# The passage between two layers of a decode kernel: one load moved ahead, one load reshaped, and idle matmuls added

## The chip, the cores and the metric

The kernel runs on one core of a Trainium2 chip. The metric is the device time of one execution in microseconds. A core has five engines with instruction streams of their own: TensorE (PE in the profile, with its weight loads as PEld), VectorE (DVE), ScalarE (ACT), GpSimd (POOL) and SyncE (SP). Sixteen DMA engines bring data from the device's memory (HBM) into the on-chip memory SBUF; here SP issues most of the transfers and ACT a few. TensorE writes its results into PSUM. Engines wait for each other, and for transfers, by semaphores.

## The reference

The reference is one decode step (one token) through two layers that use the same weights and the same caches. A layer is attention over a cache of 8192 keys and values with 32 heads, then an MLP with ReLU; each works on the layer-normed input and adds to the residual.

```python
B, Sq, D = 1, 1, 640
H, Sk, Dh = 32, 8192, 128        # caches: (1, 32, 8192, 128), f32, one for K and one for V
Dff = 1728

def _A_ref(x, k_cache, v_cache, wq, wo):
    q = (x @ wq).reshape(B, Sq, H, Dh).transpose(0, 2, 1, 3)
    scores = einsum("bhqd,bhkd->bhqk", q, k_cache) * (Dh ** -0.5)
    o = einsum("bhqk,bhkd->bhqd", softmax(scores), v_cache)
    return o.transpose(0, 2, 1, 3).reshape(B, Sq, H * Dh) @ wo

def _B_ref(x, w1, w2):
    return maximum(x @ w1, 0) @ w2

x = A_x
x = x + _A_ref(_layernorm(x), A_k_cache, A_v_cache, A_wq, A_wo)
x = x + _B_ref(_layernorm(x), B_w1, B_w2)
x = x + _A_ref(_layernorm(x), A_k_cache, A_v_cache, A_wq, A_wo)   # same caches, same weights
x = x + _B_ref(_layernorm(x), B_w1, B_w2)
```

K and V of one head are 4 MB each, 268 MB for all heads. They don't fit on chip, so almost all of them is read once in each layer.

## The kernel before, in words

**Heads and their data.** Layer 1 takes the heads 0 to 31 in order. Layer 2 takes 31 down to 24 first, then the others (`HEADS`). K and V come in units of 32 KB to 6 MB, laid out in memory one after the other in the order in which they are loaded. Some units of the heads 29, 30 and 31 stay on chip from layer 1 to layer 2 (`kept`).

**The ring and the planner.** `ring` is one large SBUF tile. `place` finds room for the next unit, `pump` issues loads on SP's queue as long as there is room, and `release` (called behind the last matmul that reads a piece) frees the room and calls `pump`. So loads run ahead of the computing by what the ring holds. When `pump` has issued the last unit of a layer it also issues W2's blocks 0 to 7 into `by_parts`, an area behind the ring.

**Other tiles that are lent.** Between the layers four units of head 29 are loaded into tiles that serve something else at other times: `load_beside(0)` into `mix` (864 KB), `load_beside(1)` into `wct` (320 KB), `load_beside(2)` and `load_beside(3)` into the two halves of `by_parts` (1280 KB each). Each is issued on SP's queue where the last reader of the tile stands in the program (lines 887 to 909).

**One head.** `begun` computes the scores (`scores`, line 494; the query is spread over a small tile by `spread_column`, line 482). `largest` (line 506) and `exponentials` (lines 511 to 520) form the softmax's numerators: a reduction on VectorE, a small matmul, a second reduction, and the exponential on ScalarE into the tile "p". `turn` (line 527) transposes them on VectorE, `values` (line 545) multiplies them with V, and `output` (lines 562 to 586) gathers one column. Work that isn't urgent (queries of the next group, the output projection) is put between by `side_work`.

**The MLP between the layers.** `mlp` starts from the last head's output `o`. The hidden row is completed by a product with `mix` (line 645), copied out (into `hr` and `hr_2`), turned into columns `hT`, and multiplied with W2 in 14 blocks of up to 128 rows (`product`, line 861, through `times_rows`, line 463). Block 13 has 64 rows (`W2_LAST`). In layer 1 the blocks 8 to 13 are loaded late, since their room has to come free: 8 and 9 into `mix` after line 820, the others into `by_parts` over the blocks 0 to 3, each after the product that reads the overwritten block (lines 866 to 868). Then x2, the input of layer 2, is formed (line 918). It is turned into columns (`columns`, line 923), the first head's query is computed from it without waiting for the layer norm (line 929), turned (line 941) and spread (line 942), and the scores of layer 2's first head begin. The norm's mean (`mean`, line 343) and deviation follow beside them.

**Idle matmuls.** `in_wait(n)` (line 387) is a matmul of n columns whose result nobody reads. The kernel before has a few of them, at places where TensorE waits.

What sets the order is the program as written: each engine runs its instructions in program order, and SP issues its loads in program order, each when its semaphores allow.

Of the kernel before, what the change touches and what calls it, by code (L numbers as in the profile page):

```python
# [10 lines left out]
F32 = mybir.dt.float32  # L11
# [4 lines left out]
P = 128  # L16
# [96 lines left out]
W2_MORE = [(SLOTS, 10), (10, 12), (12, 13), (13, FB)]  # L113
W2_LAST = 2 * (F_ROWS[2] - P * F_TILES)


@with_exitstack
def decode_kernel(ctx: ExitStack, tc: tile.TileContext, x, kv, wq, wo, wqo, w1, w2, out):
# [33 lines left out]
    def w2_block(L, b):  # L152
        if b < SLOTS:
            return w2_t[:, b]
        if L:
            return w2_rest[0][:, b - SLOTS]
        return mix[:, (b - SLOTS) * D :][:, :D] if b < 10 else w2_t[:, b - 10]
# [20 lines left out]
    def pump():  # L178
        while todo:
# [21 lines left out]
        n = (FB - SLOTS) * D // 8  # L201
        if not w2_rest:
            at = place(1, (0, None), n)
            if at is not None:
                w2_rest.append(ring[:, 8 * at : 8 * (at + n)].rearrange("p (b d) -> p b d", d=D))
                for a, b in W2_MORE:
                    part_of_w2(a, b, w2_rest[0][:, a - SLOTS : b - SLOTS])

    def part_of_w2(a, b, where):
        rows = W2_LAST if a == FB - 1 else P  # L210
        part = w2[P * D * a : P * D * b].rearrange("(p b d) -> p b d", p=P, d=D)
        nc.sync.dma_start(where[:rows], part[:rows])
# [129 lines left out]
    def mean(pt, s):  # L342
        nc.tensor.matmul(pt[:, 5:6], all_rows, s, start=True, stop=True)

    def less_mean(pt, cols):
        m = work.tile([P, 1], F32, name="ln_m")
        nc.vector.tensor_scalar(m, pt[:, 5:6], 1.0 / D, 0.0, op0=ALU.mult, op1=ALU.add)
# [306 lines left out]
    def attention_and_mlp(L, xr, s, before=None):  # L654
# [112 lines left out]
        for where, h in enumerate(heads):  # L767
# [49 lines left out]
    def mlp(L, o, last, xp, ph):  # L817
# [3 lines left out]
        if L == 0:  # L821
            part_of_w2(SLOTS, 10, mix[:, : 2 * D].rearrange("p (b d) -> p b d", d=D))
# [4 lines left out]
        hr = wct.rearrange("p c d -> p (c d)")[:, : 2 * P]  # L827
# [51 lines left out]
        for g in range(2):  # L879
# [3 lines left out]
                sel[:, 2 + g : 3 + g],  # L883
# [3 lines left out]
        if L == 0:  # L887
            load_beside(1, wct.rearrange("p c d -> p (c d)"), NB * P)
# [4 lines left out]
            hT[: 2 * half, nb + 1 : nb + 2], pj[: 2 * half, 1:2], 0.0, 0.0, op0=ALU.max, op1=ALU.add  # L893
# [28 lines left out]
        in_wait(64)  # L922
        pt = columns(x2)
        cols = work.tile([P, NB], F32, name="x_cols")
# [14 lines left out]
        mean(pt, s2)  # L939
        turned = ps_m.tile([P, 512], F32, name="acc")  # L940
        nc.tensor.matmul(turned[:, :1], row, one_of_each, start=True, stop=True)
# [35 lines left out]
def _laid_out(A_x, A_k_cache, A_v_cache, A_wq, A_wo, B_w1, B_w2):  # L977
# [21 lines left out]
    for b, f in enumerate(_hidden_rows()):  # L999
        w2[f >= 0, b] = np.asarray(B_w2)[f[f >= 0]][:, _COLS]  # L1000

# [13 lines left out]
        "w2": np.concatenate([w2[:, a:b].reshape(-1) for a, b in W2_PARTS + W2_MORE]),  # L1015
# [25 lines left out]
```

## Time and profile before

| | us |
|---|---|
| median of 3 runs | 1348.46 |
| lowest, highest | 1348.38, 1349.58 |
| the profiled execution | 1348.99 |
| its span, first to last instruction | 1347.2 |
| TensorE busy (matmuls) | 893.9 (66%) |
| VectorE busy | 297.2 (22%) |
| ScalarE busy | 58.5 (4%) |
| mean granted clock of TensorE | 0.794 |
| moved by DMA | 573.05 MB, mean 425 GB/s |

How to read the profile: times are in microseconds from the first instruction. The page shows the busy share of each engine in 40 equal slices, the clock granted to TensorE in tenths of full speed, and what the DMA engines moved in GB/s. The chain that ended last is followed back from the last instruction, at each step to what released it. In a view by stretches a row shows the stretch, its length, the busy time of PE, PEld, DVE, ACT and POOL with their instruction counts, then the granted clock, the DMA engines' busy share and GB/s. In the timeline a row shows start, length, engine, line, operation and tiles, how many instructions are merged, and in brackets the idle time before and what ended it.

The passage from layer 1 to layer 2 lies at about 690 to 710 us: the last head's output column is there at 692.6 us (line 586), x2 at 703.4 (line 918), and the first scores of layer 2 begin at 707.0 (line 494).

### The profile page before, as it was taken

What the parts mean: (1) busy time and instruction counts of PE and PEld (TensorE: products, weight loads), DVE (VectorE), ACT (ScalarE), POOL (GpSimd) and SP (SyncE); (2) the same over time, 40 slices, a digit from 0 to 9 for tenths busy, and PEclk for the clock granted to TensorE, in tenths of its full rate; (3) what the DMA queues carried; (4) which work ended last, traced back from release to release, by engine and by line L of the source; (5) the groups of instructions that cost most, each with busy time, mean ns of one, the idle gap of its engine ahead of it and who ended that gap; (6) DMA issues with size and microseconds to landing.
All of it is one profiled execution on the core that took longest, in us unless ns stands there. A gap on an engine that the chain in (4) does not pass through costs nothing.

```text
span 1347.2 us, 13967 instructions
## 1 busy us (share of the span) xinstructions
PE 893.9 (66%) x6092; PEld 271.7 (20%) x6092; DVE 297.2 (22%) x979; ACT 58.5 (4%) x147; POOL 2.9 (0%) x10
## 2 busy tenths in 40 slices
PE   5463676757657657576788666667576775767667
PEld 2121121211112112122243211212122121112123
DVE  2120131211212112122123322122121212212222
ACT  0000000000000000000000000000000000000000
POOL 0000000000000000000000000000000000000000
PEclk9776797888777778778798887678768778687789
DMA  9999999999999999999999999999999999999997
GB/s 398 434 427 431 435 441 428 425 429 440 431 433 424 432 437 426 433 423 421 429 364 410 435 432 434 430 435 426 435 436 426 437 429 431 435 429 430 426 427 330
DMA packets 24277, 573.05 MB, mean 425 GB/s; under 512 B 2836, under 2 KB 2968, under 8 KB 6168
## 3 DMA queue, kind: packets, MB, share of 16 engines
q1 hardware_dynamic: 21192, 530.62, 92.0%
q10 hardware_dynamic: 3024, 41.53, 7.3%
q8 instruction: 48, 0.79, 0.2%
q14 instruction: 13, 0.11, 0.0%
HBM read 572.15 MB, written 0.00 MB: 425 GB/s over the span
## 4 chain that ended last, share of the span: by engine, by line
DMA 66%; PE 27%; DVE 4%; ACT 1%; issue 1%; SPq 0%; ACTq 0%; DVEq 0%
DMA ring<-in_kv 63%; PE outs L545 10%; PE ps L494 10%; DMA ring<-in_w 2%; DVE p L566 1%; DVE h_t L506 1%; ACT p L520 1%; PE px L632 1%; PE pm L511 1%; PE acc L463 1%; PE pm L532 1%; PE px L421 1%; DMA both_t<-in_kv 1%; PE pm L579 1%; DVE p L527 1%
## 5 line engine op out<-in xcount | busy, mean ns | idle before, releaser
L545 PE MATMUL outs<-ring,p 128*4 128x512 f32 (+2 forms) x2160 | 345.5, 764 | 175.2 <-DMA ring<-in_kv 105.9
L494 PE MATMUL ps<-ring,spread_q 128*32 128x512 f32 (+3 forms) x2088 | 327.6, 723 | 122.4 <-DMA ring<-in_kv 121.7
L506 DVE TENSOR_REDUCE h_t<-ps 128x1 f32<-128x512 f32 x64 | 44.3, 692 | 385.2 <-PE ps L494 385.1
L494 PEld LDWEIGHTS ps<-ring,spread_q 128*32 128x32 f32 x2088 | 66.3, 125 | 255.6 <-issue 168.7
L545 PEld LDWEIGHTS outs<-ring,p 128*4 128x4 f32 x2160 | 49.0, 94 | 339.5 <-issue 198.5
L520 ACT ACTIVATE p<-ps,h_t 128x512 f32<-128x512 f32 x63 | 43.3, 687 | 1180.6 <-DVE h_t L512 1180.6
L527 DVE STREAM_TRANSPOSE p<-p 128x128 f32<-128x128 f32 x256 | 79.8, 312 | 63.6 <-ACT p L520 57.0
L579 PE MATMUL pm<-ones,p 128*128 128x1 f32 (+1 forms) x128 | 25.7, 270 | 97.4 <-DVE p L566 97.4
L562 DVE TENSOR_SCALAR p<-outs,ind 128x128 f32<-128x128 f32 x64 | 22.4, 351 | 284.0 <-PE outs L545 284.0
L566 DVE SCALAR_TENSOR_TENSOR p<-outs,ind,p 128x128 f32<-128x128 f32 x188 | 66.0, 351 | 6.7
L511 PE MATMUL pm<-ident,h_t 128*128 128x128 f32 x128 | 32.3, 335 | 40.4 <-DVE h_t L506 40.3
L579 PEld LDWEIGHTS pm<-ones,p 128*128 128x128 f32 x128 | 20.3, 199 | 164.0 <-DVE p L566 163.1
L632 PE MATMUL px<-w_t,wct 128*128 128x448 f32 (+1 forms) x80 | 45.8, 659 | 0.0
L532 PEld LDWEIGHTS pm<-ind,h_t 128*128 128x128 f32 x128 | 27.0, 263 | 79.8 <-issue 79.8
L433 DVE TENSOR_SCALAR q_row<-px,ln_r 128x128 f32<-128x128 f32 x56 | 19.5, 348 | 95.5 <-PE ps L494 54.6
L511 PEld LDWEIGHTS pm<-ident,h_t 128*128 128x128 f32 x128 | 19.8, 194 | 88.6 <-DVE h_t L506 86.8
L535 DVE RECIPROCAL h_t<-pm 128x1 f32<-128x1 f32 x64 | 10.7, 168 | 99.3 <-PE pm L532 99.3
L532 PE MATMUL pm<-ind,h_t 128*128 128x1 f32 x128 | 32.5, 323 | 0.0
L421 PE MATMUL px<-both_t,ln_xc 128*32 128x512 f32 x140 | 30.8, 706 | 0.0
L435 PEld LDWEIGHTS px<-sel,q_row 128*128 128x128 f32 x112 | 20.0, 223 | 37.5 <-DVE q_row L433 30.9
L463 PE MATMUL acc<-both_t,o_cols 128*32 128x160 f32 x488 | 27.0, 372 | 0.0
L512 DVE TENSOR_REDUCE h_t<-pm 128x1 f32<-128x128 f32 x64 | 18.7, 292 | 35.0 <-PE pm L511 35.0
(126 smaller groups left out, 227.3 us busy)
## 6 DMA issues: line engine op xcount, KB each, us to landing
ring<-in_kv SPq DMA_DIRECT2D x50, 6144.0 KB, 35.2
ring<-in_kv SPq DMA_DIRECT2D x24, 4096.0 KB, 30.3
ring<-in_kv SPq DMA_DIRECT2D x29, 2048.0 KB, 28.9
both_t<-in_wqo ACTq DMA_DIRECT2D x12, 2560.0 KB, 24.6
ring<-in_kv SPq DMA_DIRECT2D x4, 5120.0 KB, 33.6
ring<-in_kv SPq DMA_DIRECT2D x9, 1024.0 KB, 24.0
ring<-in_kv SPq DMA_DIRECT2D x4, 1280.0 KB, 10.7
ring<-in_w SPq DMA_DIRECT2D x4, 1280.0 KB, 26.8
```

What stands on the lines that cost most here:

```text
L421: nc.tensor.matmul(pq[32 * strip : 32 * strip + 32], xc[:, c : c + 1].to_broadcast([P, 32]), wq_t[:, c], start=c < 4, stop=c in (1, 2, 3, ...
L463: nc.tensor.matmul(acc[32 * g : 32 * g + 32, :DR], col.to_broadcast([col.shape[0], 32]), wt[:, g * DR : (g + 1) * DR], start=first, stop=last,
L494: nc.tensor.matmul(hd.ps[32 * g : 32 * g + 32, c : c + n], spread_q[:, 3 - r : 35 - r], tile_of[:, at + g * n : at + (g + 1) * n], start=f ...
L506: nc.vector.tensor_reduce(hd.nm, hd.ps, AX.X, ALU.max, negate=True)
L511: nc.tensor.matmul(pt[:, :P], hd.nm.to_broadcast([P, P]), ident, start=True, stop=True)
L520: nc.scalar.activation(hd.p, hd.ps, AF.Exp, bias=hd.low, scale=scale, accum_out=hd.l)
L527: nc.vector.transpose(hd.all_p[:, b * P : (b + 1) * P], hd.p[:, b * P : (b + 1) * P])
L532: nc.tensor.matmul(pt[:, :1], hd.l.to_broadcast([P, P]), ind[:, 4:5], start=True, stop=True)
L545: nc.tensor.matmul((hd.out if r0 < 2 else hd.out_2)[32 * g : 32 * g + 4, r0:r1].rearrange("p r d -> p (r d)"), hd.all_p[:, 32 * i : 32 * i ...
L566: nc.vector.scalar_tensor_tensor(oc, hd.out[:, r], ind[:, r : r + 1], oc, op0=ALU.mult, op1=ALU.add)
L579: nc.tensor.matmul(pt[:, :n], part, mask.to_broadcast([P, n]), start=i == 0, stop=i == len(parts) - 1,)
L632: nc.tensor.matmul(pt[:, :n], wct[:, c], w1_t[:, c, f : f + n], start=(c == 0), stop=(c == NB - 1),)
```

## The change

Four things are changed.

1. The unit of head 29 that goes into `wct` (320 KB) is issued by `pump` right behind W2's first eight blocks, while layer 1 still runs, and no longer in `mlp` behind the small products. `hr`, which was in `wct`, moves into a tile "p".
2. W2's last block is stored as 128 partitions of half a row instead of 64 partitions of a whole row. Its product becomes four matmuls with 64 rows each, of which two read the partitions 0 to 63 and two 64 to 127; the last hidden rows are computed into both halves of `hT`, by four small matmuls instead of two. In layer 1 the blocks 12 and 13 come in one load of 480 KB, issued after block 3's product; in layer 2 they stay two loads. The array in memory holds W2 twice, one for each layer's order of parts.
3. Idle matmuls in the passage: 256 columns instead of 64 ahead of `columns(x2)`, 128 new ones behind it, 64 new ones behind the query's turn. The mean's matmul and the turn's matmul are widened from 1 to 64 equal columns.
4. Idle matmuls of 512 columns in the first five heads of layer 2, between the exponentials and the transposes.

```diff
-W2_MORE = [(SLOTS, 10), (10, 12), (12, 13), (13, FB)]
+W2_MORE = [[(SLOTS, 10), (10, 12), (12, FB)], [(SLOTS, 10), (10, 12), (12, 13), (13, FB)]]
+def w2_at(b):
+    return min(b * D, (FB - 1) * D + D // 2)
...
                 for a, b in W2_PARTS[:: 1 - 2 * layer]:
-                    part_of_w2(a, b, w2_t[:, a:b])
+                    part_of_w2(layer, a, b, by_parts[:, a * D :])
+                if layer == 0:
+                    load_beside(1, wct.rearrange("p c d -> p (c d)"), NB * P)
...
-    def part_of_w2(a, b, where):
-        rows = W2_LAST if a == FB - 1 else P
-        part = w2[P * D * a : P * D * b].rearrange("(p b d) -> p b d", p=P, d=D)
-        nc.sync.dma_start(where[:rows], part[:rows])
+    def part_of_w2(L, a, b, where):
+        part = w2[L, P * w2_at(a) : P * w2_at(b)].rearrange("(p m) -> p m", p=P)
+        nc.sync.dma_start(where[:, : w2_at(b) - w2_at(a)], part)
...
-    def mean(pt, s):
-        nc.tensor.matmul(pt[:, 5:6], all_rows, s, start=True, stop=True)
+    def mean(pt, s, n=1):
+        nc.tensor.matmul(
+            pt[:, 64 : 64 + n], all_rows, s.to_broadcast([P, n]), start=True, stop=True
+        )
...
-            elif where >= H - 3:
+            elif where >= H - 3 or L and where < 5:
                 in_wait(512)
...
-        hr = wct.rearrange("p c d -> p (c d)")[:, : 2 * P]
+        hr = work.tile([P, D], F32, name="p")[:, : 2 * P]
...
         def product(b):
-            rows = W2_LAST if b == FB - 1 else P
-            first, end = b == early[0], b == FB - 1
-            times_rows(po, w2_block(L, b)[:rows], hT[:rows, b : b + 1], first, end)
+            wt = w2_block(L, b)
+            if b < FB - 1:
+                times_rows(po, wt, hT[:, b : b + 1], b == early[0], False)
+                return
+            for g in range(4):
+                rows = slice(W2_LAST * (g // 2), W2_LAST * (g // 2 + 1))
+                nc.tensor.matmul(
+                    po[32 * g : 32 * g + 32, :DR],
+                    hT[rows, b : b + 1].to_broadcast([W2_LAST, 32]),
+                    wt[rows, g % 2 * DR : (g % 2 + 1) * DR],
+                    start=False,
+                    stop=True,
+                    skip_group_check=True,
+                )
...
-            for part in () if L else W2_MORE[1:]:
+            for part in () if L else W2_MORE[0][1:]:
                 if b == part[1] - 11:
-                    part_of_w2(*part, w2_t[:, part[0] - 10 : part[1] - 10])
+                    part_of_w2(0, *part, by_parts[:, (part[0] - 10) * D :])
...
-        for g in range(2):
+        for g in range(4):
             nc.tensor.matmul(
                 pj[half * g : half * g + half, 1:2],
                 hr_2[:, P : P + half],
-                sel[:, 2 + g : 3 + g],
+                sel[:, 2 + g % 2 : 3 + g % 2],
...
-        if L == 0:
-            load_beside(1, wct.rearrange("p c d -> p (c d)"), NB * P)
...
-        in_wait(64)
+        in_wait(256)
         pt = columns(x2)
+        in_wait(128)
...
-        mean(pt, s2)
+        mean(pt, s2, 64)
         turned = ps_m.tile([P, 512], F32, name="acc")
-        nc.tensor.matmul(turned[:, :1], row, one_of_each, start=True, stop=True)
+        nc.tensor.matmul(
+            turned[:, :64], row, one_of_each.to_broadcast([P, 64]), start=True, stop=True
+        )
+        in_wait(64)
         spread_column(turned[:, :1])
```

More of the change, by code (lines that the diff above doesn't have):

```diff
@@ L154, in w2_block @@
             return w2_t[:, b]
+        n = w2_at(b + 1) - w2_at(b)
         if L:
[L156 to L157 removed]
+            return w2_rest[0][:, (b - SLOTS) * D :][:, :n]
+        return mix[:, (b - SLOTS) * D :][:, :n] if b < 10 else by_parts[:, (b - 10) * D :][:, :n]
     def place(layer, u, n):
@@ L821, in mlp @@
         if L == 0:
-            part_of_w2(SLOTS, 10, mix[:, : 2 * D].rearrange("p (b d) -> p b d", d=D))
+            part_of_w2(0, SLOTS, 10, mix)
         pd = ps_m.tile([P, 512], F32, name="pm")
@@ L892, in mlp @@
         nc.vector.tensor_scalar(
-            hT[: 2 * half, nb + 1 : nb + 2], pj[: 2 * half, 1:2], 0.0, 0.0, op0=ALU.max, op1=ALU.add
+            hT[:, nb + 1 : nb + 2], pj[:, 1:2], 0.0, 0.0, op0=ALU.max, op1=ALU.add
         )
@@ L1014, in _laid_out @@
         "w1": np.asarray(B_w1).reshape(NB, P, DFF).transpose(1, 0, 2),
-        "w2": np.concatenate([w2[:, a:b].reshape(-1) for a, b in W2_PARTS + W2_MORE]),
+        "w2": np.array(
+            [
+                np.concatenate([w2[:, w2_at(a) : w2_at(b)].reshape(-1) for a, b in W2_PARTS + more])
+                for more in W2_MORE
+            ]
+        ),
     }
```

13 lines of the change are left out of this document (8 added, 5 removed).

## The prediction

> **What bounds the kernel now.** I read the page's slices and its chain of waits first, then the middle (the passage from layer 1 to layer 2) by stretches, then its transfers, its chain in order of time and its instructions.
>
> ```profile
> span 1347.2 us, 13967 instructions
> GB/s 398 434 427 431 435 441 428 425 429 440 431 433 424 432 437 426 433 423 421 429 364 410 435 432 434 430 435 426 435 436 426 437 429 431 435 429 430 426 427 330
> DMA 66%; PE 27%; DVE 4%; ACT 1%; issue 1%; SPq 0%; ACTq 0%; DVEq 0%
> ```
>
> The chain that ended last is two thirds waits for transfers, and the transfers run at about 430 GB/s in every slice but the first, the last, and two in the middle (364 and 410). So time can be won only where the transfers run below that rate; a faster TensorE elsewhere is worth nothing. The stretches of the middle (last two numbers: share of the DMA engines that is busy, and GB/s):
>
> ```profile
> 690.00:695.50 5.50, 4.62 (x66) 3.24 (x62) 2.05 (x9) 0.74 (x3) 0.00 (x0) 1.00 0.61 227
> 695.50:698.50 3.00, 3.00 (x75) 2.39 (x68) 1.04 (x7) 0.00 (x0) 0.00 (x0) 1.00 0.84 256
> 698.50:701.00 2.50, 2.39 (x32) 1.27 (x36) 0.16 (x1) 0.00 (x0) 0.56 (x1) 1.00 0.96 362
> 701.00:702.00 1.00, 0.73 (x14) 0.34 (x6) 0.00 (x0) 0.00 (x0) 0.00 (x0) 1.00 0.91 246
> 702.00:704.00 2.00, 1.51 (x20) 0.81 (x20) 0.39 (x2) 0.00 (x0) 0.00 (x0) 1.00 1.05 424
> 704.00:710.00 6.00, 5.45 (x38) 2.71 (x41) 1.25 (x8) 0.00 (x0) 0.21 (x1) 0.51 1.02 425
> 710.00:716.00 6.00, 4.70 (x67) 1.96 (x59) 1.61 (x5) 0.87 (x2) 0.34 (x1) 0.92 0.98 331
> 716.00:760.00 44.00, 33.60 (x294) 11.29 (x294) 14.94 (x49) 2.34 (x6) 0.00 (x0) 0.91 1.01 432
> ```
>
> Lost against 430 GB/s, as length x (430 - rate) / 430: 2.60 us, 1.21, 0.40, 0.43, then almost nothing to 710, and 1.38 in 710 to 716: some 6.1 us in all. From 716 on nothing is lost (432), so a microsecond of transfer won before 716 is carried to the end. The transfers themselves are issued on SP's queue (then what line 212's issues waited for, in total, times and longest, and line 212's times to landing):
>
> ```profile
> 669.83 0.33 SPq L212 DMA_DIRECT2D ring<-in_w  x1
> 693.90 0.33 SPq L212 DMA_DIRECT2D mix<-in_w  x1
> 696.07 1.46 SPq L212 DMA_DIRECT2D ring<-in_w  x3
> 697.62 0.53 SPq L216 DMA_DIRECT2D wct<-in_kv  x1
> 703.27 0.33 SPq L216 DMA_DIRECT2D ring<-in_kv  x1
> 708.97 0.33 SPq L187 DMA_DIRECT2D ring<-in_kv  x1
> SPq L212 <- DMA ring<-in_kv: 33.8, 8, 4.6
> ...
> DMA to landing us min/median/max: 4.5/19.2/27.7
> ```
>
> After 669.83 nothing can be issued until TensorE has freed the mix tile (693.90), hence the idle from 690. The three loads of line 212 are W2's blocks 10 and 11, block 12, and block 13 with 64 rows. The issue at 708.97 is the first refill of the ring: the transfers fall short at 710 because it comes late. What stands before it is this chain (start, length, what), and, in the last two lines, the chain at the kernel's end:
>
> ```profile
> 696.50 5.69 DMA ring<-in_w
> 702.23 0.48 PE px L463 x8
> 702.73 0.52 PE px L463 x8
> 703.36 0.40 DVE xr L918 x2
> 704.69 1.06 PE px L929 x10
> 705.75 0.52 PE pm L343 x2
> 706.27 0.47 PE acc L941 x2
> 707.00 1.92 PE ps L494 x8
> ...
> 1328.03 15.05 DMA ring<-in_w
> 1343.12 0.99 PE px L463 x16
> ```
>
> Rows for the prices at full clock and for the gaps that the idle products fill come next, then two stretches of equal length for the granted clock (the number before the DMA share):
>
> ```profile
> 660.06 1.92 PE L494 MATMUL ps<-ring,spread_q 128*32 128x512 f32 x16 [1.11 <-DMA ring<-in_kv]
> 663.12 1.02 PE L390 MATMUL pt<-w_t,ident 128*128 128x512 f32 x2
> 679.05 0.38 PE L343 MATMUL pm<-x_s,sel 128*128 128x1 f32 x2
> 703.14 0.43 PE L390 MATMUL pt<-w_t,ident 128*128 128x64 f32 x2
> 703.80 0.38 PE L331 MATMUL pm<-sel,xr 128*128 128x4 f32 x2 [0.23 <-DVE xr L918]
> 727.70 1.63 PE L545 MATMUL outs<-ring,p 128*4 128x512 f32 x8 [1.60 <-DVE p L527]
> ...
> 700.72:704.13 3.41, 2.65 (x40) 1.52 (x39) 0.39 (x2) 0.00 (x0) 0.00 (x0) 1.00 1.03 368
> 673.41:676.82 3.41, 2.21 (x14) 0.97 (x14) 1.62 (x5) 0.00 (x0) 0.00 (x0) 1.00 1.02 432
> ```
>
> **The change part by part.** *K29's part for wct.* 320 KB, 0.33 MB, 0.76 us at 430 GB/s. Its issue leaves 697.62 and stands behind 669.83. There SP may wait for an earlier landing first, as line 212 does up to 4.6 us, so I put it near 674.7; behind it SP has nothing before 693.90, 19 us later, so that wait delays nobody. The load joins a full queue and fills 0.76 us of the idle after 690. It frees the same 0.76 us after 697.62. The hidden products' copy moves from wct to the tile "p", whose last reader has ended before the copy's own input is there: nothing.
>
> *W2's last block on 128 partitions, in layer 1 together with block 12.* One load of 480 KB in place of 320 and 160, one issue of 0.5 us less on SP. Around 701 the engines are busy 0.91 of the time and move only 246 GB/s, while the 64-row load is among those in flight; 698.5 to 702 loses 0.83 us. I take 0.6 of it as won (ends 0 and 0.83). Landing: blocks 10 and 11 land 4.5 us after 696.07, at 700.57 (the shortest time to landing of line 212); 480 KB behind them are 1.14 us, so 701.7 in place of 702.19, and block 13 need not be waited for again. Its product then ends some 0.5 us sooner. Ends: 0.6 sooner; 0.4 later, if the joint load lands only when block 13 did. Two more small products for the hidden rows (line 880) lie in the wait for W2: nothing. In layer 2 the blocks stay apart, the bytes of the last load stay the same, and the chain there is one of landings up to 1343.08: nothing (ends: 0.3 us either way, about the wait before block 13's product).
>
> *Idle products in the middle.* The clock is at 0.51 from 704 to 710. At full clock the four links of the chain cost: scores 0.96 for 1.92 (half of the row at 660.06), the sum 0.38 for 0.52, the turn 0.38 for 0.47, the query 0.6 for 1.06 (between half of it and the whole; nearer to half, since scores halve): 2.3 for 3.97, so 1.65 won. Against it: 256 columns instead of 64 take some 0.68 (between 0.43 and 1.02 by columns) from 703.14 and so end when the columns of x2 start, at 703.80: 0.05. 128 columns ahead of the query's first product, in a gap of some 0.25: 0.05. 64 columns in place of one in two products: by 0.43 against 0.38, 0.05 each. The last 64 lie behind the turn while DVE spreads the query: nothing. Altogether 0.2 lost, 1.45 won.
>
> Does the clock hold? The stretch 700.72 to 704.13 was followed by half clock although TensorE counts as busy for 2.65 us; 673.41 to 676.82 was followed by full clock with 2.21 us. The first consists of 40 short matmuls, the second of 14 that include long ones: so long streams count, not instructions. The change adds 192 + 128 + 3 x 64 columns, by the difference of 1.02 and 0.43 over 448 columns some 0.67 us of streams, and W2's earlier landing moves products forward. I take it that the clock holds.
>
> *First refill.* 0.5 + 1.45: issued near 707.0 instead of 708.97. Data follow an issue by some 1.6 us (693.90, and the rate rises at 695.5): 708.6. The older loads run out at about 710.2 now, and after the change 0.76 + 0.6 sooner, at 708.8. So the refill is just in time and the 1.38 us of 710 to 716 go. Had the chain not moved, the 0.76 and 0.6 would be idle there instead.
>
> *Idle products in layer 2's first five heads.* 512 columns, 1.02 us, in a gap of 1.60 us between the largest and the values: hidden at full clock. In the first head the gap is smaller, and I allow 0.5 us. Nothing is won by them, since 716 to 760 loses nothing. What could be late is the refill that is issued after the third head; the load before it, and that load's time from issue to landing:
>
> ```profile
> 733.40 0.33 SPq L187 DMA_DIRECT2D ring<-in_kv  x1
> 750.31 0.33 SPq L187 DMA_DIRECT2D ring<-in_kv  x1
> ...
> ring<-in_kv SPq DMA_DIRECT2D x1, 4096.0 KB, 23.0
> ```
>
> The load of 733.40 lands at 756.4; the data of the refill of 750.31 are there by 751.9 (1.6 us, as above), 4.5 us before. After the change both move by 2 to 3 us, so 0.5 us more in the first head is covered by this margin.
>
> **The sum.** 0.76 + 0.6 + 1.38 = 2.74 us. The profiled execution took 1348.99 us (span 1347.2 and 1.8 around it) and would take 1346.25; the median of the three runs is 0.53 below it, so I forecast 1345.7, 0.20% less. A difference within 0.2% (2.7 us) is about what a measurement of this kernel can tell from no change.
>
> [...]
>
> **Rivals.** *The clock falls all the same.* For it: the same clock state came after quite unlike stretches, and I know the limit only between two rows. Then the chain wins 0.5 - 0.2 = 0.3 us at most, the refill's data come at 710.3, and the older loads end at 708.8: 1.5 us idle, which is the 1.38 of now and a little more. Won is what the refill won, 0.3 to 0.6 us: 1347.9 to 1348.2. Against it: 0.67 us more streams in 3.41.
>
> *The idle products stand in the way (slower).* Place: TensorE's path from x2 to the refill after layer 2's third head, if the clock stays at half. Price: three products of 512 columns take 2 x 1.02 each, 6.1 us, all of it exposed; the chain wins only 0.3. The refill is then issued at 756.1 and its data come at 757.7, while the loads before it end at 756.4 less the 0.45 that the first refill won: 1.7 us idle, so 1.3 more than now, 1349.7. If those in the middle are exposed too (0.68, 0.51 and three of 0.43, less the one of 0.43 that is there now, a second time for the half clock: up to 1.6 us), 1351.3. It decides from some 4.5 us of delay by the third head. For it: the row at 727.70 takes 1.63 us for eight matmuls of 512 columns, which take 0.96 at 660.06, so half clock does come up in these heads. Against it: the gap of 1.60 us in that very row, which takes most of a product even so.
>
> *The transfer was hidden anyway.* The 0.76 us of wct and the 0.6 come back as idle at 710 if the refill is issued after 707.2; with a chain shortened by 1.45 alone (W2 lands as before) it is 707.5, and 0.3 us are lost: 1346.0.
>
> **How the numbers follow.** All three terms: 0.70; own range 1344.8 to 1346.6 (the ends of W2's term, 0.3 at the end, and the third rival 0.05 inside it); the bound of 0.2% lies in it, at 1345.8, and I give 0.50 to below it and 0.25 to above. Clock falls: 0.14, within 0.2%. Idle products in the way: 0.11, of it 0.05 beyond 1351.2, the upper end of that rival's price. Faster 0.50, same 0.45, slower 0.05. The range, 1344.6 to 1348.2, takes in the first rival and leaves the second out.
>
> **What would show it.** Right: wct's load near 675; 690 to 695.5 above 227 GB/s by some 60; clock 1.00 from 704 to 710; the first refill near 707; 710 to 716 near 430; the last landing 2.7 us sooner. Wrong: a clock of 0.5 anywhere from 700 to 710, a refill after 707.5, or any stretch from 716 to 760 clearly below 430.

## The result, and the profile after

| | before | after |
|---|---|---|
| median of the runs made side by side, us | 1349.09 (1348.0 to 1351.73, 10 runs) | 1346.1 (1345.34 to 1348.12, 10 runs) |
| the profiled execution, us | 1348.99 | 1346.93 |
| its span, us | 1347.2 | 1345.1 |

The ratio is 0.9976 with a 95% interval of 0.9966 to 0.9986: 3.2 us less, between 1.9 and 4.6. The kernel is faster, by about as much as the forecast said (1345.7, which was 2.8 below the median then known).

The head of the page of the changed kernel (span, GB/s in 40 slices, the chain by engine):

```profile
span 1345.1 us, 14004 instructions
...
GB/s 396 434 427 433 436 438 421 440 423 443 426 432 436 426 436 428 429 428 418 429 377 427 433 431 435 429 439 420 435 439 427 435 428 430 439 425 432 428 426 327
...
DMA 68%; PE 25%; DVE 4%; ACT 1%; issue 1%; SPq 0%; ACTq 0%; DVEq 0%
```

Nothing outside the passage has changed: its two weak slices went from 364 and 410 GB/s to 377 and 427, and the last slice still shows 327. The same view by stretches as before, now of the changed kernel (clock, DMA share and GB/s stand last):

```profile
690.00:695.50 5.50, 4.63 (x66) 3.27 (x62) 2.06 (x9) 0.74 (x3) 0.00 (x0) 1.00 0.72 273
695.50:698.50 3.00, 3.00 (x79) 2.39 (x72) 1.03 (x7) 0.00 (x0) 0.00 (x0) 1.00 0.96 311
698.50:702.00 3.50, 3.32 (x46) 1.76 (x46) 0.16 (x1) 0.00 (x0) 0.55 (x1) 1.00 1.05 362
702.00:704.00 2.00, 2.00 (x30) 1.17 (x22) 0.52 (x3) 0.00 (x0) 0.00 (x0) 1.00 0.91 364
704.00:710.00 6.00, 5.89 (x52) 2.34 (x51) 1.13 (x8) 0.00 (x0) 0.55 (x1) 1.00 1.02 422
710.00:716.00 6.00, 4.76 (x64) 2.42 (x68) 3.16 (x12) 0.87 (x2) 0.00 (x0) 1.00 1.04 432
716.00:760.00 44.00, 35.34 (x314) 12.10 (x306) 14.79 (x48) 2.34 (x6) 0.00 (x0) 0.96 1.01 431
```

With the rule of the prediction, length x (430 - rate) / 430, the losses are 2.01, 0.83, 0.55, 0.31 and 0.11 us, then nothing: 3.8 in all where it was 6.1. So this trace wins 2.3 us, where 2.74 were forecast. What came: the clock stays at 1.00 from 704 to 710, and the hole of 710 to 716 (331 GB/s) is gone. What did not come is in 698.5 to 704. There the forecast left 0.26 us lost (0.83 - 0.6 + 0.03), and 0.86 are; from 702 to 704 the rate even fell from 424 to 364.

The loads on SP's queue in the changed kernel's timeline:

```profile
674.79 0.33 SPq L223 DMA_DIRECT2D wct<-in_kv  x1
693.89 0.33 SPq L219 DMA_DIRECT2D mix<-in_w  x1
696.05 0.84 SPq L219 DMA_DIRECT2D ring<-in_w  x2
698.51 0.33 SPq L223 DMA_DIRECT2D ring<-in_kv  x1
...
702.72 0.33 SPq L223 DMA_DIRECT2D ring<-in_kv  x1
706.97 3.37 SPq L193 DMA_DIRECT2D ring<-in_kv  x3
```

The load into wct goes out at 674.79, the load into mix as late as before, and the first refill at 706.97, 2.0 us sooner. The chain in order of time (start, length, what), and the end of the kernel in the last two lines:

```profile
696.56 5.17 DMA ring<-in_w
...
701.77 0.48 PE px L472 x8
702.25 0.41 PE px L874 x8
702.65 0.63 PE pt L399 x2
...
704.23 0.55 PE px L948 x10
704.78 0.36 PE pm L350 x2
...
705.16 0.45 PE acc L960 x2
...
705.88 1.05 PE ps L503 x8
...
1325.12 16.00 DMA ring<-in_w
...
1341.16 0.48 PE px L472 x8
```

W2's last load lands at 701.73, 0.46 us sooner, and its product follows at once (lines 472 and 874 are times_rows and the new four matmuls). Query, sum, turn and scores take 2.41 us where they took 3.97. W2's landing at the end is at 1341.12, 1.96 us sooner than 1343.08.

### The profile page after: what moved, and what is told of

It reads as the page before. It is cut to its first block, busy times and chain, and to the rows that moved or that the text cites. A ratio compares the mean times of both kernels' runs of the same rounds, so it can differ in the third digit from the quotient of the medians.

```text
span 1345.1 us, 14004 instructions
## 1 busy us (share of the span) xinstructions
PE 893.8 (66%) x6114; PEld 270.4 (20%) x6114; DVE 297.3 (22%) x979; ACT 58.5 (4%) x147; POOL 2.9 (0%) x10
## 4 chain that ended last, share of the span: by engine, by line
DMA 68%; PE 25%; DVE 4%; ACT 1%; issue 1%; SPq 0%; ACTq 0%; DVEq 0%
DMA ring<-in_kv 66%; PE outs L554 10%; PE ps L503 9%; DMA ring<-in_w 2%; DVE p L575 1%; ACT p L529 1%; PE px L641 1%; DVE h_t L515 1%; PE px L430 1%; PE pm L520 1%; PE pm L541 1%; DMA both_t<-in_kv 1%; PE acc L472 1%; PE pm L588 1%; PE px L444 1%
## 5 line engine op out<-in xcount | busy, mean ns | idle before, releaser
L503 PE MATMUL ps<-ring,spread_q 128*32 128x512 f32 (+3 forms) x2088 | 323.5, 712 | 115.0 <-DMA ring<-in_kv 114.3
L430 PE MATMUL px<-both_t,ln_xc 128*32 128x512 f32 x140 | 40.0, 898 | 0.0
L472 PE MATMUL acc<-both_t,o_cols 128*32 128x160 f32 x488 | 24.1, 342 | 0.0
```

Of the source, the lines that this page charges most:

```text
L430: nc.tensor.matmul(pq[32 * strip : 32 * strip + 32], xc[:, c : c + 1].to_broadcast([P, 32]), wq_t[:, c], start=c < 4, stop=c in (1, 2, 3, ...
L472: nc.tensor.matmul(acc[32 * g : 32 * g + 32, :DR], col.to_broadcast([col.shape[0], 32]), wt[:, g * DR : (g + 1) * DR], start=first, stop=last,
L503: nc.tensor.matmul(hd.ps[32 * g : 32 * g + 32, c : c + n], spread_q[:, 3 - r : 35 - r], tile_of[:, at + g * n : at + (g + 1) * n], start=f ...
```

## The experiments

The kernels were run in three groups, each group against the kernel before on the same chip (its medians there: 1349.3, 1349.36 and 1349.29 us). The theory was that three terms add up: wct 0.76 us, W2's last rows 0.6, and the first refill 1.38, the last only if the clock holds. The rivals were that a term is hidden, and that the idle products alone, or the clock alone, do it all.

The table puts the runs side by side. "Refill" is the time on SP's queue from the issue of the load into mix to the issue of the first refill, which takes out that single executions reach the passage up to 1 us apart. The stretches are those of the fence above, at fixed times. Put at the same distance from the load into mix in every trace (from 3.9 us ahead of it to 22.1 behind), the kernel before moves 329 GB/s, the changed kernel 367 and 373 in its two traces, and after_no_wct 376. Up to the first refill after, after_again and after_no_heads_idle run the same instructions, and their refills still differ by 0.51 us (13.08, 13.31 and 13.59): two single traces can't show less than that.

| kernel | ratio to before (95%) | median, us | refill, us | clock 704 to 710 | GB/s 698.5 to 702 | GB/s 710 to 716 |
|---|---|---|---|---|---|---|
| before | 1 | 1349.3 | 15.07 | 0.51 | 328 | 331 |
| wct_alone | 1.0005 (0.9996 to 1.0013) | 1349.4 | 13.93 | 0.56 | 353 | 383 |
| mid_idle_alone | 0.9995 (0.9981 to 1.0009) | 1347.7 | 13.52 | 1.00 | 330 | 426 |
| w2_alone | 0.9987 (0.9977 to 0.9997) | 1347.28 | 14.73 | 0.72 | 389 | 374 |
| heads_idle_alone | 0.9999 (0.9990 to 1.0008) | 1348.2 | 15.65 | 0.50 | 337 | 316 |
| after_no_wct | 0.9979 (0.9970 to 0.9988) | 1345.97 | 13.32 | 1.00 | 413 | 425 |
| after_no_mid_idle | 0.9984 (0.9975 to 0.9992) | 1346.91 | 13.67 | 0.72 | 406 | 348 |
| after_no_heads_idle | 0.9983 (0.9971 to 0.9994) | 1346.65 | 13.59 | 1.00 | 410 | 398 |
| after_no_w2 | 0.9988 (0.9978 to 0.9998) | 1348.19 | 15.55 | 0.51 | 340 | 322 |
| after | 0.9976 (0.9966 to 0.9986) | 1346.1 | 13.08 | 1.00 | 362 | 432 |
| after_again | 0.9973 (0.9962 to 0.9983) | 1346.2 | 13.31 | 1.00 | 394 | 416 |
| after_b2_sooner | 0.9976 (0.9966 to 0.9986) | 1346.56 | 13.63 | 1.00 | 392 | 393 |
| after_chain_1us | 0.9979 (0.9970 to 0.9987) | 1346.5 | 13.76 | 1.00 | 398 | 384 |
| after_w2_apart | 0.9968 (0.9955 to 0.9981) | 1345.8 | 13.17 | 1.00 | 408 | 430 |

### Each part alone, on the kernel before

**The load into wct alone.**

```diff
+                if layer == 0:
+                    load_beside(1, wct.rearrange("p c d -> p (c d)"), NB * P)
...
-        hr = wct.rearrange("p c d -> p (c d)")[:, : 2 * P]
+        hr = work.tile([P, D], F32, name="p")[:, : 2 * P]
...
-        if L == 0:
-            load_beside(1, wct.rearrange("p c d -> p (c d)"), NB * P)
```

> Only K29's part for wct is issued ahead (hr in tile "p"); nothing else is changed. Theory (the ledger: a transfer moved ahead is given back where the first refill is late): 690 to 695.5 rises from 227 to some 275 GB/s, the refill stays near 709, 710 to 716 falls from 331 to some 280 GB/s, and the last landing and the time move by less than 0.3 us. Rival (the parts add up): the time falls by 0.76 us, and 710 to 716 stays at 331.

Measured: 1.0005 (0.9996 to 1.0013), so a gain of more than 0.5 us (0.0004 of 1349) is outside the interval, and 0.76 was the term. The stretch from 690 to 695.5 does rise, from 227 to 286 GB/s. The theory's other signs did not come: the refill is issued at 707.25 and not near 709, and 710 to 716 rises to 383 GB/s instead of falling to 280. Two things account for the sooner refill. W2's last rows land 7.79 us behind the load into mix (8.29 in the kernel before), and the clock falls at 704.76, 11.44 us behind it (10.23 before), so that the query's product (line 929) still runs at full clock, 0.64 us where it was 1.06. The traced execution is also the fastest of the 11 (1347.4, where the median is 1349.4). So the runs show that this load alone wins next to nothing; that its gain is given back at a late refill, this trace doesn't show.

**The idle products of the middle alone.**

```diff
-        in_wait(64)
+        in_wait(256)
         ... columns(x2) ...
+        in_wait(128)
...
-        mean(pt, s2)
+        mean(pt, s2, 64)
-        nc.tensor.matmul(turned[:, :1], row, one_of_each, start=True, stop=True)
+        nc.tensor.matmul(turned[:, :64], row, one_of_each.to_broadcast([P, 64]), start=True, stop=True)
+        in_wait(64)
```

> Only the idle products of the passage (256, 128, 64 columns, the two widened products) are added. Theory: the clock is 1.00 from 704 to 710, the refill comes near 707.5, 710 to 716 rises to 420 or more, the time falls by 1.2 to 1.4 us. Rival (the clock falls all the same, or W2's earlier landing is needed to hold it): clock near 0.5 in 704 to 710, refill at 709, no change.

Measured: 0.9995 (0.9981 to 1.0009). In its trace the clock holds and the refill comes 1.55 us sooner behind the load into mix; 710 to 716 rises to 426 GB/s. W2's 64-row load lands at 701.92, 8.68 us behind the load into mix (8.29 in the kernel before), so the clock holds here without an earlier landing. The time is undecided: the median is 1.6 us below the before of its group, but of the 11 runs two took 1352.17 and 1355.41, and they carry the ratio. So the mechanism is shown, its worth alone is not.

**W2's last rows alone.**

```diff
-W2_MORE = [(SLOTS, 10), (10, 12), (12, 13), (13, FB)]
+W2_MORE = [[(SLOTS, 10), (10, 12), (12, FB)], [(SLOTS, 10), (10, 12), (12, 13), (13, FB)]]
... w2_at, part_of_w2(L, ...), the last block as four 64-row matmuls, four small products
```

> Only W2's last block is reshaped and joined with block 12 in layer 1. Theory: W2's last landing near 701.7 instead of 702.7, 698.5 to 702 loses some 0.4 us less, the clock still falls, the refill comes near 708.4, and of the gain at most 0.5 us is left. Rival (it is the reshaped load that holds the clock): clock 1.00 from 704 to 710 and the time lower by 1.5 us or more.

Measured: 0.9987 (0.9977 to 0.9997), 1.75 us less (0.4 to 3.1): the one part that is faster by itself. By the median that is more than the 0.5 us expected, which the interval takes in. Its trace shows two things. The rate from 698.5 to 702 goes from 328 to 389 GB/s; and the clock is at half for one window of 3.42 us, where the kernel before has 0.51 over all of 704 to 710. (In the traces of before and after the granted clock is 1.00 or 0.50, and it keeps each value for a multiple of 3.41 us: in before 0.50 from 704.13 to 710.95, 6.82 us, then 1.00 up to 728.02, 17.07 us. Such a step of 3.41 us is called a window here.) The landing expected near 701.7 came at 702.09, 8.73 us behind the load into mix, so measured that way it is not sooner than before (8.29). Three windows of its trace, in the columns of the stretches:

```profile
699.25:702.66 3.41, 2.37 (x32) 0.99 (x34) 0.00 (x0) 0.00 (x0) 0.00 (x0) 1.00 1.05 399
702.66:706.07 3.41, 2.59 (x34) 1.73 (x30) 1.04 (x6) 0.00 (x0) 0.00 (x0) 1.00 0.99 413
706.07:709.49 3.42, 3.38 (x18) 1.05 (x22) 0.60 (x5) 0.00 (x0) 0.55 (x1) 0.50 1.01 423
```

In the kernel before the fall came at 704.13, here at 706.07, after a window that the short matmuls fill by 2.59 us. So the query's product still runs at full clock (0.64 us). Whether the edit moved the fall or the window only happened to start there, one trace can't tell. The first row shows besides that busy time alone does not set the clock: 2.37 us were followed by full clock, 2.59 by half.

**The idle products of layer 2's first heads alone.**

```diff
-            elif where >= H - 3:
+            elif where >= H - 3 or L and where < 5:
                 in_wait(512)
```

> Only the 512-column idle products in layer 2's first five heads are added. Theory: transfers from 716 on run at 430 GB/s with and without them; no change (under 0.3 us in the trace). Rival (they win what the runs won beyond the profile, 3.0 us against 2.1, by keeping refills of the first heads in time in those executions that take 1351 us): no change in the trace, but the upper end of the times falls by 2 us.

Measured: 0.9999 (0.9990 to 1.0008). No effect is seen in the time. The upper end (1351.65 of 11 runs, 1353.54 of 33 before) settles nothing about the rival. The trace moves 426 GB/s from 716 to 760 where the kernel before has 432; after_no_w2, the other trace whose refill comes over 15.5 us behind the load into mix, has 426 too.

### The change with one part undone

Each of the next four is the changed kernel with one of the edits above taken back.

**Without the load into wct ahead** (the diff of wct_alone, reversed).

> The changed kernel, with K29's part for wct issued behind the small products again. Theory: the refill is as early as with it (near 707.0) and 710 to 716 stays near 430; 690 to 695.5 falls to 227; the time is 0.76 us above the changed kernel's, last landing near 1341.9. Rival (the load matters only through the older loads, which end later by it): no change, because the refill no longer is just in time but early.

Measured: 0.9979 (0.9970 to 0.9988), beside 0.9976 and 0.9973 for the changed kernel: nothing is missed. Where the 0.76 us went is read from the stretches and the queue of this kernel, here

```profile
690.00:695.50 5.50, 4.63 (x76) 3.24 (x64) 2.07 (x9) 0.74 (x3) 0.00 (x0) 1.00 0.68 265
695.50:698.50 3.00, 3.00 (x72) 2.30 (x64) 1.18 (x7) 0.00 (x0) 0.24 (x1) 1.00 0.95 304
698.50:702.00 3.50, 3.11 (x44) 1.32 (x36) 0.00 (x0) 0.00 (x0) 0.31 (x1) 1.00 1.05 413
702.00:704.00 2.00, 2.00 (x28) 1.41 (x24) 0.56 (x3) 0.00 (x0) 0.00 (x0) 1.00 0.98 417
700.50:701.50 1.00, 0.78 (x16) 0.46 (x10) 0.00 (x0) 0.00 (x0) 0.00 (x0) 1.00 1.11 435
```

beside those of the changed kernel in the execution that is nearest in time (after_again; the load into mix goes out at 693.31 there, at 693.11 here):

```profile
690.00:695.50 5.50, 4.63 (x75) 3.31 (x69) 2.07 (x9) 0.74 (x3) 0.00 (x0) 1.00 0.76 284
695.50:698.50 3.00, 2.79 (x68) 2.13 (x60) 1.18 (x7) 0.00 (x0) 0.05 (x1) 1.00 0.96 340
698.50:702.00 3.50, 3.39 (x50) 1.62 (x49) 0.00 (x0) 0.00 (x0) 0.50 (x1) 1.00 1.05 394
702.00:704.00 2.00, 2.00 (x30) 1.25 (x23) 0.56 (x3) 0.00 (x0) 0.00 (x0) 1.00 0.96 385
700.50:701.50 1.00, 0.96 (x22) 0.57 (x18) 0.00 (x0) 0.00 (x0) 0.00 (x0) 1.00 1.03 358
```

Ahead of 698.5 the moved load wins (5.5 x 19 + 3 x 36) / 430 = 0.49 us. Behind it, down to 716 (412 and 416 GB/s against 419 and 425 in the last two stretches), (3.5 x 19 + 2 x 32 + 6 x 7 + 6 x 9) / 430 = 0.53 us are lost. Over 690 to 716 both kernels move 373 GB/s. With the load in its old place 698.5 to 704 runs at 413 to 417 GB/s, with the load moved ahead at 385 to 394. Where the loss lies differs between executions: after_no_heads_idle, which has the load ahead too, moves 410 and 395 GB/s there, and loses (6 x 36 + 6 x 32) / 430 = 0.95 us from 704 to 716 instead.

**Without the idle products of the middle.**

> The changed kernel without the idle products of the passage. Theory: the clock falls to half near 704, the refill comes near 708.4, 710 to 716 falls to 300 or less, the time is 1.5 to 2.2 us above the changed kernel's. Rival (W2's earlier landing is enough to hold the clock): clock 1.00, refill near 706.9, no change.

Measured: 0.9984 (0.9975 to 0.9992), which lies 1.1 to 1.5 us above the changed kernel's two ratios, with intervals that overlap. The clock is at half for one window (0.72 as mean from 704 to 710), the refill comes 13.67 us behind the load into mix, and 710 to 716 falls to 348 GB/s, 1.14 us lost there. Those are the size and the place of the refill's term, most of it. It is less than expected (refill near 708.4, 300 GB/s or less, 1.5 to 2.2 us), because in this trace the clock falls at 705.43 only, when the query and its turn are done.

**Without the idle products of the heads.**

> The changed kernel without the idle products in layer 2's first five heads. Theory: no change (under 0.3 us in the trace, the same spread of times). Rival (they keep later refills in time): a stretch between 716 and 760 below 425 GB/s, and the time 0.5 to 1 us higher.

Measured: 0.9983 (0.9971 to 0.9994), 0.9 to 1.3 us above the changed kernel's two ratios, with intervals that overlap. The runs alone can't tell that from the effect of the middle's products; the trace puts none of it on these. From 716 to 760 it moves 432 GB/s at a clock of 0.83, the changed kernel 431 at 0.96: the clock rises and the transfers do not notice. What this trace loses lies from 704 to 716 (394 and 398 GB/s), and the first of the products that are missing here begins at 713.34 in the changed kernel. In the changed kernel's timeline (start, length, instruction, in brackets the idle time before it) the added product sits in the gap:

```profile
723.39 1.02 PE L399 MATMUL pt<-w_t,ident 128*128 128x512 f32 x2
725.15 1.04 PE L554 MATMUL outs<-ring,p 128*4 128x512 f32 x8 [0.74 <-DVE p L536]
```

The values still wait for VectorE, 0.74 us where it was 1.60. That is hidden, as costed.

**Without W2's last rows.**

> The changed kernel with W2's last block as 64 rows and blocks 12 and 13 apart. Theory: W2's last landing near 702.7, refill near 707.5, 698.5 to 704 loses some 0.6 us more, the time 0.5 to 0.8 us above the changed kernel's. Rival (the shape of that load costs nothing; only the chain counts): the time equal within 0.2 us.

Measured: 0.9988 (0.9978 to 0.9998), 1.6 to 2.0 us more than the changed kernel's two ratios, with intervals that overlap: nominally more than the 0.6 us of that term. Four windows of its trace show what else is lost:

```profile
700.75:704.17 3.42, 2.77 (x36) 1.66 (x32) 0.56 (x3) 0.00 (x0) 0.00 (x0) 1.00 0.94 348
704.17:707.58 3.41, 3.41 (x22) 2.15 (x24) 0.93 (x7) 0.00 (x0) 0.00 (x0) 0.50 1.03 432
707.58:710.99 3.41, 3.41 (x22) 0.96 (x18) 0.16 (x1) 0.00 (x0) 0.55 (x1) 0.50 0.86 284
710.99:714.41 3.42, 2.60 (x34) 0.95 (x30) 0.90 (x2) 0.00 (x0) 0.00 (x0) 1.00 0.94 344
```

All idle products are there, and the clock falls all the same, for two windows. W2's last rows land later (702.27, 9.0 us behind the load into mix, against 7.8 in the changed kernel), TensorE waits for them inside the window from 700.75, and what the idle products add (2.77 us busy against 2.65 in the kernel before) does not hold the clock. The refill is then issued 15.55 us behind the load into mix and the hole of the kernel before is back (284 and 344 GB/s). The first rival of the prediction, that the clock falls all the same, is what this execution does.

A late landing alone does not bring the fall: mid_idle_alone has the same 64-row load and the same idle products, its last rows land 8.7 us behind the load into mix, and its clock holds. Its windows start elsewhere. The first two rows below are its windows. The third is after_b2_sooner (described further down), whose windows lie nearly as in after_no_w2: with W2 reshaped the last landing is 8.4 us behind the load into mix, TensorE is busy for 3.23 us, and the clock holds.

```profile
698.74:702.16 3.42, 2.82 (x40) 1.30 (x36) 0.00 (x0) 0.00 (x0) 0.20 (x1) 1.00 1.02 336
702.16:705.57 3.41, 3.39 (x38) 2.22 (x30) 1.00 (x6) 0.00 (x0) 0.00 (x0) 1.00 0.98 412
...
700.76:704.17 3.41, 3.23 (x48) 1.83 (x40) 0.56 (x3) 0.00 (x0) 0.00 (x0) 1.00 0.93 376
```

So without W2's edit it seems to hang on where the windows start whether the clock holds. The run times of after_no_w2 fit that: four lie from 1345.82 to 1346.06, as the changed kernel's do, seven from 1348.07 to 1350.0, and none between. The traced execution, 1348.6, is one of the seven; none of the four was traced, so this is not shown.

### Where the load's gain went, and how much the refill may be late

These four ran in one group.

**The changed kernel once more**, unaltered.

> The changed kernel once more, unaltered, on the same chip as the three below, so that they can be compared with it. Expected: 3 us under the kernel before.

Measured: 0.9973 (0.9962 to 0.9983). It confirms the result.

**The load behind wct's sooner.** My explanation after the second group was that the hole at 698.5 to 704 opens because the next load, into the second half of by_parts (`load_beside(2)`), is issued too late. It waits for the product of block 7. Here the products 4 to 7 go ahead of the small products in layer 1.

```diff
+        if L == 0:
+            for b in then:
+                product(b)
+            load_beside(2, by_parts[:, 4 * D :], 4 * D)
+            then = ()
...
-            if b == SLOTS:
+            if b == (SLOTS if L else 10):
                 r1 = spread_of_rows(ss)
...
-            if b == 7:
-                load_beside(2, by_parts[:, 4 * D :], 4 * D)
```

> The changed kernel, in layer 1 with W2's products 4 to 7 ahead of the small products of the last hidden rows, so that the 1280 KB load that overwrites their blocks is issued near 697.9 instead of 698.5 (the norm's second sum goes behind product 9). Theory (the 0.76 us of wct is lost again because this load comes too late to follow W2's last one): 698.5 to 704 rises from 363 GB/s to 400 or more, and if the first refill is still in time the time falls by 0.5 to 0.7 us against the changed kernel. Rival (the hole is there for another reason, the start of every load after an idle stretch): 698.5 to 704 stays near 363, no change.

Measured: 0.9976 (0.9966 to 0.9986). That load goes out 4.20 us behind the load into mix (693.38 and 697.58) instead of 4.61 (693.31 and 697.92 in after_again), and the hole is as it was:

```profile
698.50:702.00 3.50, 3.26 (x46) 1.85 (x46) 0.75 (x4) 0.00 (x0) 0.55 (x1) 1.00 1.05 392
702.00:704.00 2.00, 2.00 (x30) 1.13 (x22) 0.48 (x3) 0.00 (x0) 0.00 (x0) 1.00 0.98 386
700.50:701.50 1.00, 1.00 (x19) 0.72 (x18) 0.00 (x0) 0.00 (x0) 0.00 (x0) 1.00 0.92 344
```

So 0.4 us on that issue changes nothing, and my explanation is not supported. The deepest microsecond, 700.5 to 701.5, has 358 GB/s in after_again, 344 here and 347 in after_w2_apart, while after_no_wct has 435, but so nearly has after_no_heads_idle, with the load ahead (428). Where it is deep, the engines are busy for 0.87 to 1.03 of it, so packets run slowly there rather than not at all. What slows them is open.

**The chain longer by one product.** It measures what a late refill costs.

```diff
         mean(pt, s2, 64)
+        in_wait(512)
         turned = ps_m.tile([P, 512], F32, name="acc")
```

> The changed kernel with one more idle product of 512 columns ahead of the query's turn, so on the chain to the first refill, and at full clock. Theory of the prediction (the refill is just in time, its slack 0.2 us): refill 0.6 to 0.9 us later, 710 to 716 loses 0.4 to 0.7 us, the time rises by as much. Rival (the refill is early, since the older loads end later than predicted): refill as much later, 704 to 716 within 5 GB/s of the changed kernel's, no change.

Measured: 0.9979 (0.9970 to 0.9987). The product takes 0.91 us on the chain (704.45 to 705.36), but the turn behind it takes 0.17 where it takes 0.45 in after_again, and the refill is later by only 0.45 us: 13.76 behind the load into mix instead of 13.31. The rows:

```profile
693.14 0.33 SPq L219 DMA_DIRECT2D mix<-in_w  x1
...
706.90 3.37 SPq L193 DMA_DIRECT2D ring<-in_kv  x3
```

In 710 to 716 the rate is 384 GB/s instead of 416, (416 - 384) x 6 / 430 = 0.45 us. That is the theory's price, but it is no more than the same instructions differ by: after_no_heads_idle has a refill 13.59 us behind the load into mix and 398 GB/s. From 690 to 716 this trace moves 370 GB/s and after_again 373, which is 26 x 3 / 430 = 0.18 us, and its span is the shorter one (1344.0 and 1344.2). The medians differ by 0.3 us, inside both ranges. So what a refill that is half a microsecond late costs is not shown here.

**W2's last two blocks as two loads**, both on 128 partitions.

```diff
-W2_MORE = [[(SLOTS, 10), (10, 12), (12, FB)], [(SLOTS, 10), (10, 12), (12, 13), (13, FB)]]
+W2_MORE = [[(SLOTS, 10), (10, 12), (12, 13), (13, FB)], [(SLOTS, 10), (10, 12), (12, 13), (13, FB)]]
```

> The changed kernel with W2's block 12 and its reshaped block 13 as two loads in layer 1, issued after products 2 and 3. Theory (the 64 rows are what was slow, not the number of loads): within 0.3 us of the changed kernel. Rival (it is the joining, one landing and one issue less): time and 698.5 to 702 as without the whole of the W2 part, 1.6 us above the changed kernel.

Measured: 0.9968 (0.9955 to 0.9981), median 1345.8, nominally the fastest of all, with an interval that overlaps the changed kernel's. It moves more in its trace from 690 to 716 than any other (380 GB/s). So joining the two loads brings nothing that can be seen. After_no_w2 has two loads as well, one of them with 64 rows, and moves 340 GB/s from 698.5 to 702 where this trace moves 408: there it is the shape that counts.

## Why the prediction was right, point by point

**The limit.** Right. The differences that the traces show lie where the transfers ran below 430 GB/s, and a higher clock where they do not changed nothing (716 to 760: 432 GB/s at a clock of 0.83 in after_no_heads_idle, 431 at 0.96 in the changed kernel).

**K29's part for wct, 0.76 us.** This is the term that failed. Its issue near 674.7 (measured 674.79), that it delays nobody on SP's queue, and the rise of 690 to 695.5 (forecast some 60 GB/s, measured 46 and 57) were right, though the 227 GB/s of the one trace before was low: the five traces without the load ahead have 251 on average, after_no_wct 265 among them, the nine with it 285. The step that failed is "It frees the same 0.76 us after 697.62". Time is freed only if the loads behind run at the full rate in the room that is left, and they do not: 0.49 us won, 0.53 given back before 716. By the averages of these five and nine traces it wins (5.5 x 34 + 3 x 42) / 430 = 0.73 us ahead of 698.5. Still, from 690 to 716 the six traces that have the load ahead and both other terms move 366 to 380 GB/s, and after_no_wct 373. The rival "the transfer was hidden anyway" named the right effect at the wrong place. It looked for the idle at 710, behind a late refill; it comes between 698.5 and 716, with the refill in time, and not always in the same place. Wct_alone can't decide this, since the prediction itself has the 0.76 us idle where the chain has not moved; after_no_wct can. The runs put the term near nothing: alone its gain is below 0.5 us, and the changed kernel without it is 0.4 to 0.8 us slower with an uncertainty of more than that. I can name where it went, not why the packets are slow there.

**W2's last rows, 0.6 us.** Right in kind and roughly in size. The five traces with the 64-row load move 328, 353, 330, 337 and 340 GB/s from 698.5 to 702, the nine without it 362 to 413. Their means, 338 and 397, are 0.48 us apart over 3.5 us. A landing at 701.7 was forecast and 701.73 measured, 7.84 us behind the load into mix; in w2_alone the same load landed 8.73 us behind it, so the close hit is partly chance. The traces agree with a lower rate for the 64-row load, and no run shows what makes it lower; but the dip at 701 is not all its own: the changed kernel has 348 GB/s from 701 to 702 in after_again, w2_alone 388. What the prediction did not price is a second effect: a landing that is late in a window takes matmuls out of it. In after_no_w2 the landing at 702.27 leaves TensorE 2.77 us busy from 700.75 to 704.17, in the changed kernel the one at 701.73 leaves it 3.24 from 700.78 to 704.20. After_no_w2 lost its clock with that window; mid_idle_alone, with other window starts, did not.

**Idle products in the middle.** Right. The chain's four links took 0.55, 0.36, 0.45 and 1.05 us (forecast 0.6, 0.38, 0.38 and 0.96), 2.41 in place of 2.3, and the 256 columns 0.63 (forecast 0.68). "I take it that the clock holds" came true for the changed kernel as a whole, but with less room than it sounds. In the passage the clock held in all seven traces that have these idle products and W2's edit; of the two that have the idle products alone it held in one (mid_idle_alone) and fell in the other (after_no_w2); it fell in all five without them. The windows that were followed by half clock have 2.65 us busy (before), 2.59 (w2_alone) and 2.77 (after_no_w2). So they hold 0.76, 0.82 and 0.65 us of idle time in 3.4: the clock fell after windows with little of it. Yet busy time alone is not the measure, since 2.37 us in w2_alone were followed by full clock; that long streams count is the prediction's reading of two rows, and no run varied the streams alone. The half clock of w2_alone lasts 3.42 us and starts 1.94 us later than in the kernel before, which is no multiple of 3.41: its windows start elsewhere.

**First refill, 1.38 us.** Right: 707.0 forecast, 706.97 measured, and "just in time" as far as traces of one execution each can say. Over the table, 710 to 716 moves 416 to 432 GB/s in the five kernels that issue it at most 13.52 us behind the load into mix and 316 to 331 in the three slowest (15.07 and more); between them it falls, if not in strict order. The prediction set the point at 707.5, which is 13.6 behind. The earlier end of the older loads, 708.8 by its sum, was by the same reckoning too early by what wct gave back, which would leave the refill a little more room than thought.

**Layer 2's first heads.** Right: hidden, no gain, and no refill late (716 to 760 at 431 GB/s).

**The second rival.** Its price does not come out as written: 0.68, 0.51 and three of 0.43, less one of 0.43, are 2.05 us and not 1.6 (1.6 is what is left when the first refill's 0.45 is taken off). It did not come up, so nothing else rests on it.

**The sum.** 2.74 us were forecast. The trace gives 2.3 by the stretches, 1.96 at W2's last landing and 2.1 in span; the terms for W2 and the refill make 0.48 + 1.38 = 1.9. In after_again, whose traced execution took 1346.03 us, the six stretches lose 3.4 us instead of 6.1, so 2.7. The runs' medians differ by 3.0 and the interval, 1.9 to 4.6, holds all of these. So the time came out within 0.4 us of the forecast although one of three terms is not there. That it came so near is partly chance: the terms that the traces show make 1.9 to 2.3, and the traced execution of the changed kernel, 1346.93, is 0.8 us above its median. Whether the rest of the 3.0 is more than this spread stays open.

## What to carry to other kernels

A load that was moved into idle time won 0.49 us there in one pair of traces, and the loads behind it, which ran below 430 GB/s, gave back 0.53, so read the stretch that it leaves, not only the one it fills. The clock held in eight traces of the nine with idle matmuls in the passage and fell in all five without, and in the ninth TensorE waited for late data (702.27) inside a window: look at each window of 3.4 us, in the worst place of its start. And don't read a part's worth from one trace of each variant: here the same instructions gave refills half a microsecond apart, and in the kernels that lost the clock in the passage it fell between 10.1 and 12.7 us behind the same load.

## What was not expected of the hardware

The start of the clock's windows differs between executions (falls at 704.13 and 706.07 in the traces of before and w2_alone, 1.94 us apart where a window has 3.41). That the same matmuls keep the clock in one run and lose it in another is my reading of that and not shown: one profile of a kernel shows one case, and no kernel was traced both ways. The hole at 700.5 in some of the traces, with engines busy and 344 to 358 GB/s, is the other surprise. And at the end of layer 2, in the changed kernel,

```profile
1330.00:1336.00 6.00, 5.09 (x85) 3.59 (x76) 2.08 (x9) 0.74 (x3) 0.00 (x0) 1.00 0.97 398
1336.00:1340.00 4.00, 3.22 (x72) 2.30 (x64) 1.18 (x7) 0.00 (x0) 0.55 (x1) 1.00 0.52 201
1340.00:1341.20 1.20, 0.79 (x20) 0.46 (x22) 0.00 (x0) 0.00 (x0) 0.00 (x0) 1.00 0.06 21
```

the DMA engines are half busy for 4 us, at 201 GB/s, and almost idle for 1.2 us more, before W2's last landing at 1341.12. The first alone is 4 x (430 - 201) / 430 = 2.1 us, as much as the whole change won in its span. The kernel before has 222 GB/s in the like stretch (1338 to 1342), so neither uses it.
